# Causal triangle by matmul in two blocks, wide zero matmuls and a new order of work in a fused attention and MLP kernel

## The chip, the cores and the metric

The kernel runs on one core of one Trainium2 chip. A core has five engines that each work through their own list of instructions in order: PE (matmuls; PEld is its loading of weights), ACT (activations and copies), DVE (vector work), POOL (element-wise work, and the issue of software DMAs) and SP (here only the issue of hardware DMAs). Engines wait for each other by semaphores. The metric is the device time of one launch in microseconds (us); lower is better.

## The reference

The inputs are q, k and v of shape (4, 8, 768, 64) and two weight matrices, 512x2048 and 2048x512, all float32. For each query the reference bounds its score against each chunk of 32 keys, keeps the six best chunks among those that causality allows, and runs causal softmax attention over the keys of these chunks. A softplus MLP follows.

```python
k_min, k_max = k_chunks.min(axis=3), k_chunks.max(axis=3)
ub = sum(maximum(q * k_min, q * k_max), axis=-1)   # causal chunks only
top_chunks = argsort(ub)[..., -6:]
scores = where(sel & (pos_q >= pos_k), q @ k.T / 8, -1e9)
attn = softmax(scores)
x = (attn @ v) laid out as (3072, 512)
out = softplus(x @ w_in) @ w_out
```

## The kernel before

The work is cut into 12 blocks of 256 queries: block n is batch n // 3 and query block n % 3, so a block sees 256, 512 or 768 keys. Work on one block has these steps; the names are those of the planned operations, with n the block.

- **Loads.** k and q of block 0 come as f32 by SP's queue (`ld k0`, `ld q0`, line 352) and are cast on ACT or DVE. v of block 0, all of k, q and v of later blocks, and the weights come by POOL's software queue, which casts to bf16 on the way (line 339; w_in line 376, w_out line 383). Issuing one occupies POOL.
- **Preparation.** k and q are turned: in blocks 0 to 2 by PE transposes (`kT`, `qT`, line 471), from block 3 by DMA transposes on SP's queue (line 475). DVE takes maxima and minima of the chunks (`kx`, `kn`), `bd` lays them out, `kc`, `qc` and `qac` copy, `qpn` splits q into positive and negative parts. `ub` (lines 570, 574) is the matmul of the bounds, `mx` the six best, `raw` the mask, `mT` its transpose, `mc` its copy into extra rows beside q. Matching rows beside k (`ohk`, made by POOL as `oh` in lines 275 to 279 and spread by SP) make the score matmul add the mask.
- **Attention.** `s` (lines 687, 688) writes scores of one head against 256 keys; where those are the diagonal keys, its second matmul covers 128 queries only. `ex` (line 695) is the exponential on ACT. On the diagonal `af` (line 705, POOL) then sets to zero what lies above it. `av` (line 717) multiplies with v and a column of ones, `nm` normalizes, `oT` (line 743) or a DMA transpose (line 732) turns the result, and `xc` puts it into x.
- **MLP.** `h` (line 791), exponential `e` (796) and logarithm `ln` (801) on ACT, `y` (816), `ye` copies and `st` stores.

All instructions are put into their lists by a planner that is part of the kernel's program (`Plan.run`). Each operation has a key, and a due time: the smallest of its own key and of the due times of what follows it less durations. A loop keeps a planned time for each engine and each buffer. For each engine it takes, among those operations that could start within a tolerance (`tol`) of the earliest, the one with the smallest due time. DMAs are given a planned time of landing by a small model of the two queues. Keys, tolerances and buffer counts are the numbers in `PAR` (lines 224 to 245). What reaches the chip is the order on each engine, no times: an instruction runs as soon as its engine comes to it and its semaphores are there.

`keep_awake` (line 837) then fills PE's planned idle time in the first 45 us with matmuls of zeros (line 852), each of 128 columns, counted so that they end 60 ns before the planned start of the next real operation. They cost what the planner holds them to cost: 107 ns before 5.7 us and 55.8 ns later. A buffer pool `io` of eight tiles takes the loaded k and q.

Of the kernel before, what the change touches and what calls it, by code (L numbers as in the profile page):

```python
# [21 lines left out]
QB = 256  # L22
# [41 lines left out]

class Op:
    __slots__ = ("name", "alts", "fn", "deps", "gate", "after", "succ", "alloc", "touch", "key",
                 "rel", "packet", "port", "due", "wait", "eng", "start", "end", "done", "dma", "n", "at", "inst")


class Plan:  # L70
# [5 lines left out]
    def op(self, name, alts, fn, deps=(), alloc=(), touch=(), key=None, dma=None, gate=(), after=(), rel=0.0, packet=19.0, port=False):  # L76
        o = Op()
        o.rel, o.packet, o.port = round(rel), packet, port
# [50 lines left out]
    @staticmethod  # L129
    def home_at(pool, s, e):  # L130
        t = 0.0
        for q, x, dma in pool.ends[s]:
            t = max(t, x + (LANDED[e] if dma else 0 if q == e == "PE" else LAT[q].get(e, 150)))
        return t

    def run(self, par):
# [11 lines left out]
        ring, packet = {"SP": 0.0, "POOL": 0.0}, {"SP": 19.0, "POOL": 32.0}  # L148
# [3 lines left out]
        while ready:  # L152
# [26 lines left out]
            if o.dma:  # L179
                other = "SP" if e == "POOL" else "POOL"  # L180
                at = max(o.end + (650 if e == "SP" else 1150), ring[e], 2650.0)
                back, part = max(0.0, ring[other] - at), packet[other] / o.packet
                ring[e] = at + o.dma + min(o.dma * part, back)
                ring[other] += min(o.dma, back / part)
                packet[e] = o.packet
                o.done = ring[e] + (450 if o.packet < 100 else 1000)
                if e == "SP":
                    o.end = max(o.end, ring[e] - 3500)
            else:
                o.done = o.end  # L190
# [4 lines left out]
            for b in o.touch:  # L195
                b.left -= 1
                b.ends.append((e, o.done, bool(o.dma)))
# [22 lines left out]
def dve(n, rate=1.0):  # L220
    return n / (0.96 * rate) + 66


PAR = dict(
    dmat=3,
    dmaT=450,
    narrow=1,
    l0=1,
    over="soy",
    maskD=3,  # L230
    awake=(1.06, 45.0, 5.7),
    first=(64.42, 64.23, 29.03, 95.39),
    loads=((87.43, 130.15, 71.7), 19.14, (76.86, 12.06, 15.17), 41.22),
    tol={"PE": 0, "ACT": 0, "DVE": 0, "POOL": 2358, "SP": 0},
    alt=636,
    ohd=(229.35, 150.58),
    a=(-46.8, -33.92, -31.03, -0.05, 17.1, 24.77, 54.71, 88.7, 133.12, 175.62, 173.66, 255.42, 297.45, 469.8),
    prep=((77.31, -48.97, -81.43, 46.38), (-8.14, 24.92, -67.86, -43.68), (53.78, -16.07, -58.0, 11.26), (25.03, -41.37, -16.45, 11.23)),
    av=(-0.8, 4.76),
    ot=(12.12, 10.86),  # L240
    hlag=(8.7, 27.7, 34.1, -3.53, 34.9, 33.84, 33.54, 32.2, 25.36, -32.32, 54.03, 77.81),
    ylag=(7.32, 7.87, 25.64, 26.35, 28.67, 47.05, 47.88, 49.45, 10.02, 22.03, 47.36, 37.39),
    ahead=(3.4, 19.67, 10.64, 22.05, 12.72, 9.33, 70.63, 47.4, 103.95),
    sizes=dict(s=2, h=2, y=1, o=1, t=2, xf=2, xp=4, kT=2, io=8, kx=2, q=2, pn=2, ub=2, pt=4, osb=4, x=4, g=2, e=4, ysb=4, mT=2),
# [3 lines left out]
def make_plan(T, par):  # L248
# [19 lines left out]
    P.op("zero", [("DVE", 80)], lambda e: nc.vector.memset(T.zero, 0.0), key=-100000)  # L268
# [26 lines left out]
    chunk_rows = [P.op("c4", [("POOL", 900)], f4, [r4], key=3000)]  # L295
    mr0, bd0, kb0, vone, ohk = [], [], [], [], {}
# [11 lines left out]
    for k0, k1 in ((0, 1), (1, NBLK)):  # L308
        for h in range(2):
            o = P.op("ohk", [("SP", 450)], lambda e, k0=k0, k1=k1, h=h: rows_of(0, k0, k1, h), oh[k0:k1],  # L310
                     key=par["ohd"][k0] * 1e3, dma=300 * (k1 - k0))
# [16 lines left out]
    def load(nm, n, when, gate=()):  # L328
# [6 lines left out]
        for t in range(NT):  # L335
# [4 lines left out]
                     gate=gate, key=key, rel=key - 2000 if n > 2 else 0.0, dma=950 if n < 3 else 2050, packet=32.0, **new)  # L340
            first = first or o
            ld[nm, n, t] = o

    def load_pairs(nm, n, when):
# [4 lines left out]
        for g in range(2):  # L349
# [4 lines left out]
                     key=1e3 * when[g], dma=950, packet=29.0, alloc=[st])  # L354
# [6 lines left out]
    def load_rows(nm, n, when):  # L361

        for t in range(NT):
            st = Buf(pool["xf"])
            d = P.op(f"ld {nm}{n}.{t}", [("SP", 560)], lambda e, t=t, st=st: nc.sync.dma_start(out=st.ap, in_=rows(nm, n, t)),
                     key=1e3 * (when + 0.3 * t), dma=1000, alloc=[st])
# [5 lines left out]
    def load_w_in(when):  # L372
        for c in range(4):
# [4 lines left out]
            w_in.append(P.op(f"w_in{c}", [("POOL", 800)], f, key=1e3 * (when + 0.4 * c), dma=2550, packet=173.0, after=w_in[-1:]))  # L378

    def load_w_out(when):  # L380
        for c in range(4):
# [4 lines left out]
            w_out.append(P.op(f"w_out{c}", [("POOL", 800)], f, key=1e3 * (when + 0.4 * c), dma=2550, packet=173.0,  # L386
# [5 lines left out]
    load_pairs("k", 0, (0.0, l0[0]))  # L392
    if par["l0"] < 2:
        load_pairs("q", 0, (l0[1], l0[2]))
    else:
        load("q", 0, l0[1])
# [4 lines left out]
    for nm, x in zip("kqv", l1):  # L401
        load(nm, 1, x)
    load_w_in(li)
    for nm, x in zip("kqv", l2):
        load(nm, 2, x)
    load_w_out(lo)
    for h in range(2):
        o = P.op("ohk", [("SP", 450)], lambda e, h=h: rows_of(1, 0, NBLK, h), oh, gate=[w_out[3]], key=40000, dma=900)
        for k in range(NBLK):
            ohk[1, k, h] = o  # L410
    kb0.append(P.op("kb0", [("SP", 450)], lambda e: nc.sync.dma_start(out=T.KB[1][0:32], in_=T.KB[0][0:32]), kb0[:1],
                    gate=[w_out[3]], key=40000, dma=600))
# [7 lines left out]
    for n in range(NB):  # L420
# [11 lines left out]
        for gi, ps in enumerate(groups):  # L432
# [14 lines left out]
            by_dma, pairs, qpairs = n >= par["dmat"], n == 0, n == 0 and par["l0"] < 2  # L447
# [20 lines left out]
            def transposes(nm, buf, t, n=n, ps=ps, p0=p0):  # L468
                o = t_of(buf)
                for p in ps:  # L470
                    nc.tensor.transpose(o[:, p - p0, t * 128:(t + 1) * 128],
# [476 lines left out]
```

## Time and profile before

| | |
|---|---|
| median of 3 runs | 264.73 us (264.21 to 266.2) |
| profiled execution, its own time | 266.59 us |
| its span | 264.8 us |
| PE, ACT, DVE, POOL busy | 96%, 80%, 54%, 42% of the span |
| mean granted clock of PE | 0.994 |
| first and last matmul of an MLP (lines 791, 816) | start 36.06 us, end about 261.2 us |

The page gives shares of the span. Its tenths are 40 slices of 6.6 us each. Times inside the profile are counted from the span's start, and the profiled execution took 1.8 us more than its span; that execution was itself 1.9 us over the median. A matmul's row is longer than the time to the next one, since matmuls overlap: only distances between starts tell what one costs.

### The profile page before, as it was taken

The numbers are of one execution on the slowest core, as the hardware profiler recorded it, in microseconds if no ns is written. First come the engines' busy times: TensorE is split into PE (matmuls) and PEld (weight loads), VectorE is DVE, ScalarE is ACT, GpSimd is POOL, SyncE is SP. The second block draws the span as 40 slices with busy tenths as digits, with TensorE's granted clock in tenths as the row PEclk, the third lists the DMA queues.
The fourth block names the chain that finished last, engine by engine and source line by source line (L and its number), as shares of the span: only waits on it lengthen the run. The fifth ranks groups of instructions, "written<-read, shape, count | busy, mean of one in ns | idle before, by whom it ended". The sixth has DMA issues, their size and how long they took to land.

```text
span 264.8 us, 7039 instructions
## 1 busy us (share of the span) xinstructions
PE 255.0 (96%) x2750; PEld 197.2 (74%) x2779; DVE 142.5 (54%) x500; ACT 211.0 (80%) x372; POOL 110.8 (42%) x193
## 2 busy tenths in 40 slices
PE   8698999999999999999999999999999999999995
PEld 8698898768775677788678864777888756887744
DVE  6589961019789667447634596584582164221012
ACT  3589999988687879999687992699997885999900
POOL 8927878798318520543990263401110211310000
PEclk9799999999999999999999999999999999999999
DMA  7996999999999984699699969624440123001022
GB/s 162 161 189 90 181 196 231 155 139 190 149 136 173 132 119 89 115 129 100 73 173 150 117 88 174 173 54 120 45 82 0 42 72 99 10 2 42 0 79 79
DMA packets 114719, 29.87 MB, mean 113 GB/s; under 512 B 104544, under 2 KB 111712, under 8 KB 114688
## 3 DMA queue, kind: packets, MB, share of 16 engines
q0 software_dynamic: 74944, 13.11, 66.5%
q1 hardware_dynamic: 39744, 16.33, 33.0%
q8 instruction: 21, 0.34, 0.6%
q14 instruction: 10, 0.08, 0.1%
HBM read 27.26 MB, written 6.29 MB: 127 GB/s over the span
## 4 chain that ended last, share of the span: by engine, by line
PE 86%; DMA 5%; DVE 3%; ACT 3%; issue 1%; POOL 0%; DVEq 0%; POOLq 0%
PE ph L791 30%; PE py L816 17%; PE pt L816 9%; PE po L717 7%; PE ps L687 5%; PE py L852 4%; PE ps L688 4%; DMA io<-in_k_dram 3%; DMA x<-osb 3%; PE pt L687 2%; PE pt L688 1%; PE pt L570 1%; ACT g L801 1%; PE ph L816 1%; ACT e L796 1%
## 5 line engine op out<-in xcount | busy, mean ns | idle before, releaser
L791 PE MATMUL ph<-x,w_in_sb 128*128 128x256 bf16 x768 | 91.8, 272 | 0.0
L705 POOL TENSOR_SCALAR_AFFINE_SELECT pt<-pt 128x256 bf16<-128x256 bf16 x96 | 39.5, 419 | 112.6 <-ACT pt L695 112.1
L791 PEld LDWEIGHTS <-w_in_sb 128*128 128x128 bf16 x768 | 73.6, 98 | 11.5 <-DMA w_in_sb<-in_moe_w_in_dram 0.5
L695 ACT ACTIVATE pt<-ps 128x512 bf16<-128x512 f32 (+1 forms) x134 | 69.9, 564 | 9.4 <-PE ps L688 8.8
L796 ACT ACTIVATE e<-ph 128x512 f32<-128x512 f32 x96 | 56.3, 606 | 12.5 <-PE ph L791 11.8
L816 PEld LDWEIGHTS <-g 128*128 128x128 bf16 x400 | 37.4, 98 | 31.4 <-ACT g L801 0.5
L816 PE MATMUL py<-w_out_sb,g 128*128 128x512 bf16 x231 | 57.8, 379 | 1.5 <-ACT ysb L258 0.2
L801 ACT ACTIVATE g<-e 128x1024 bf16<-128x1024 f32 x48 | 51.1, 1072 | 1.0
L695 ACT ACTIVATE pt<-pt 128x512 bf16<-128x512 f32 (+1 forms) x58 | 32.4, 584 | 0.6 <-PE pt L688 0.6
L717 PEld LDWEIGHTS <-pt 128*128 128x128 bf16 x672 | 26.8, 97 | 5.1 <-issue 0.6
L259 DVE COPY ysb<-py 128x512 f32<-128x512 f32 x12 | 8.3, 691 | 36.9 <-PE py L816 36.9
L717 PE MATMUL po<-v,pt 128*128 128x65 bf16 x610 | 26.4, 193 | 0.3 <-DVE osb L728 0.3
L816 PE MATMUL pt<-w_out_sb,g 128*128 128x512 bf16 x108 | 26.2, 379 | 0.2
L727 DVE RECIPROCAL rec<-po 128x4 f32<-128x4 f32 x43 | 7.6, 178 | 34.9 <-PE po L717 34.6
L490 DVE TENSOR_REDUCE kx<-kT 128x32 bf16<-128x1024 bf16 x18 | 21.0, 1209 | 8.9 <-DMA kT<-io 8.9
L852 PE MATMUL py<-zero 128*128 128x128 bf16 x243 | 22.7, 245 | 1.1 <-DVE zero L268 1.1
L339 POOL DMA_DIRECT2D v<-in_v_dram x24 | 21.6, 905 | 3.8 <-DMA io<-in_q_dram 1.5
L339 POOL DMA_DIRECT2D io<-in_k_dram x22 | 20.0, 910 | 5.7 <-DMA w_in_sb<-in_moe_w_in_dram 2.2
L339 POOL DMA_DIRECT2D io<-in_q_dram x22 | 19.9, 910 | 0.7 <-PE ph L791 0.6
L728 DVE TENSOR_TENSOR osb<-po,rec 128x256 bf16<-128x256 f32 x43 | 18.2, 424 | 2.7 <-DMA x<-osb 1.3
L852 PEld LDWEIGHTS <-zero 128*128 128x128 bf16 x243 | 18.3, 111 | 1.3 <-DVE zero L268 1.1
L687 PE MATMUL ps<-qa,ka 96*128 96x256 bf16 x71 | 18.3, 273 | 0.7 <-DVE qa L259 0.7
(99 smaller groups left out, 302.5 us busy)
## 6 DMA issues: line engine op xcount, KB each, us to landing
out_dram<-ysb SPq DMA_DIRECT2D x23, 256.0 KB, 2.4
v<-in_v_dram POOLq DMA_DIRECT2D x24, 128.0 KB, 7.6
io<-in_k_dram POOLq DMA_DIRECT2D x22, 128.0 KB, 7.2
io<-in_q_dram POOLq DMA_DIRECT2D x22, 128.0 KB, 7.1
w_out_sb<-in_moe_w_out_dram POOLq DMA_DIRECT2D x4, 512.0 KB, 8.0
w_in_sb<-in_moe_w_in_dram POOLq DMA_DIRECT2D x4, 512.0 KB, 9.6
xp<-in_k_dram SPq DMA_DIRECT2D x2, 256.0 KB, 3.2
xp<-in_q_dram SPq DMA_DIRECT2D x2, 256.0 KB, 6.3
```

What stands on the lines that cost most here:

```text
L339: lambda e, t=t: nc.gpsimd.dma_start(out=into(nm, n, t), in_=rows(nm, n, t)),
L490: nc.vector.tensor_reduce(kx.ap[:, :, j].rearrange("d p (t c) -> d t p c", t=NT), kT.ap.rearrange("d p x -> d (p x)").rearrange("d (t p c ...
L687: nc.tensor.matmul(sp.ap[:, 0:QB], kk[0:nr, p, j * 128:(j + 1) * 128], qq, start=True, stop=True)
L695: lambda e, sp=sp, pt=pt, h=h, j=j, w=w: nc.scalar.activation(pt.ap[:, h, j:j + 2].rearrange("k j c -> k (j c)")[:, 0:w], sp.ap[:, 0:w], A ...
L705: nc.gpsimd.affine_select(out=d, in_=d, compare_op=ALU.is_ge, fill=0.0, base=0, channel_multiplier=-1, pattern=[[0, 2], [1, 128]])
L717: nc.tensor.matmul(o[:, u, h], pt.ap[:, h, j, c0:c0 + 128], T.V[i][:, j, 2 * p + h, :], start=(j == 0), stop=(j == t0 + u))
L728: nc.vector.tensor_tensor(osb.ap[0], o[:, :, :, 0:D], osb.ap[1].to_broadcast([128, NT, 2, D]), op=ALU.mult)
L791: nc.tensor.matmul(o[:, j], T.w_in[:, dt, ft * 128:(ft + 1) * 128], x.ap[:, dt], start=(dt == 0), stop=(dt == KDM - 1))
L796: lambda e, hb=hb, eb=eb, f2=f2: nc.scalar.activation(eb.ap[:, f2 * 512:(f2 + 1) * 512], hb.ap, ACT.Exp),
L801: lambda e, eb=eb, g=g, f4=f4: nc.scalar.activation(g.ap[:, f4 * 4:(f4 + 1) * 4].rearrange("f j c -> f (j c)"), eb.ap, ACT.Ln, bias=1.0),
L816: nc.tensor.matmul(yb.ap[:, 0:c1 - c0], g.ap[:, f, u * 128:(u + 1) * 128], T.w_out[:, f, c0:c1], start=(f == 0), stop=(f == KFF - 1))
L852: z.fn = lambda e: T.nc.tensor.matmul(T.pools["y"].homes[0][:, 0:128], T.zero, T.zero, start=True, stop=True)
```

## The change

Seven things change.

1. **Triangle.** In blocks 0 and 1 (`tri=2`) the causal triangle is added before the exponential: behind each of the two diagonal score matmuls stands a 128x128 matmul of the identity with a constant tile `tri` that holds a large negative number above the diagonal. The `af` selections of these two blocks go, 8 per block. Other blocks keep them. POOL makes `tri` from zeros that DVE writes.
2. **Software loads.** In the plan no software load of blocks 0 to 2 begins ahead of 3.3 us (`rel=3300`). No wait in the kernel goes with it.
3. **Zero matmuls.** They take 512 columns, and 128 where 512 no longer fit. The tile of zeros has 512 columns.
4. **Model of the DMAs.** The class `Rings` takes the place of a few lines: packets of two queues share the engines, a software transfer waits for hardware ones issued before it for up to 3.3 us, and a transfer lands later than its last packet by an amount of its own (`land`): 0.45 us for f32 loads, 1.3 to 3.2 us for software loads (`SKEW` for block 0), 2.8 us for transposes. It sets only the order.
5. **Due times.** `tweak` adds to an operation's due time by its name. Among some 170 entries: tri -1.15, `ld q1.0` -3.0, `ld k1.1` -30.76, `ld v0.0` +19.38, vone +18.65, oh +19.6.
6. **Numbers.** All keys are new, POOL's tolerance goes from 2.36 us to 9.85 us.
7. **Buffers.** `io` goes from eight tiles to five.

A loader `load_both` and its transposes are added too; with `both=0` nothing calls them.

```diff
+class Rings:
+    def __init__(self):
+        self.t, self.q, self.on = 0.0, {"POOL": [], "SP": []}, {"POOL": False, "SP": False}
+        self.slots = []
+    def run(self, until, ends):
+        t, q, on = self.t, self.q, self.on
+        pair = (("POOL", "SP"), ("SP", "POOL"))
+        while True:
+            nxt = 1e18
+            for e, f in pair:
+                if q[e] and not on[e]:
+                    x = q[e][0]
+                    late = x[1] + 3300.0
+                    if x[1] <= t and (t >= late or not q[f] or q[f][0][5] > x[5]):
+                        on[e] = True
...
+            per = sum(q[e][0][4] for e in act)
+            if len(act) == 2:
+                per += q["SP"][0][0].pen
...
+    def add(self, o, now):
+        self.run(max(now, self.t), [])
+        e = "POOL" if o.eng == "POOL" else "SP"
...
+        self.q[e].append([o, max(o.end + (1150 if e == "POOL" else 650), 2650.0), n, 0, o.packet, o.end])
...
@@ Plan.run
+        for o in topo:
+            o.due += 1e3 * par["tweak"].get(o.name, 0.0)
...
-                at = max(o.end + (650 if e == "SP" else 1150), ring[e], 2650.0)
...
-                o.done = ring[e] + (450 if o.packet < 100 else 1000)
+                for x, y in rings.add(o, t - 2500.0):
+                    y += x.land
...
@@ PAR
+    tri=2,
-    first=(64.42, 64.23, 29.03, 95.39),
-    loads=((87.43, 130.15, 71.7), 19.14, (76.86, 12.06, 15.17), 41.22),
-    tol={"PE": 0, "ACT": 0, "DVE": 0, "POOL": 2358, "SP": 0},
+    first=(93.07, 179.76, 83.28, 50.42),
+    loads=((108.73, 142.65, 46.12), 80.17, (59.6, 38.68, 238.83), 28.45),
+    tol={"PE": 27, "ACT": 222, "DVE": 0, "POOL": 9847, "SP": 0},
-    a=(-46.8, -33.92, -31.03, -0.05, 17.1, 24.77, 54.71, 88.7, 133.12, 175.62, 173.66, 255.42, 297.45, 469.8),
-    prep=((77.31, -48.97, -81.43, 46.38), (-8.14, 24.92, -67.86, -43.68), (53.78, -16.07, -58.0, 11.26), (25.03, -41.37, -16.45, 11.23)),
-    av=(-0.8, 4.76),
-    ot=(12.12, 10.86),
+    a=(-77.41, -53.74, -51.32, -48.9, 23.04, 68.67, 100.01, 106.1, 141.55, 250.15, 284.3, 344.37, 488.94, 634.54),
+    prep=((58.7, -107.29, -20.36, 94.1), (40.17, 56.54, -119.0, -8.26), (-6.33, -38.41, -55.12, -66.62), (19.56, -17.84, 30.35, -49.53)),
+    av=(-16.58, 36.73),
+    ot=(-42.75, -53.14),
...
@@ make_plan
+    if par["tri"]:
+        t0_ = P.op("tri0", [("DVE", 100)], lambda e: nc.vector.memset(T.tri, 0.0), key=2000)
+        tri_ = [P.op("tri", [("POOL", 430)], lambda e: nc.gpsimd.affine_select(
+            out=T.tri, in_=T.tri, compare_op=ALU.is_ge, fill=NEG, base=0, channel_multiplier=-1, pattern=[[1, 128]]), [t0_], key=8000), ident]
...
-                     gate=gate, key=key, rel=key - 2000 if n > 2 else 0.0, dma=950 if n < 3 else 2050, packet=32.0, **new)
+                     gate=gate, key=key, rel=key - 2000 if n > 2 else 3300.0 if par["l0"] == 1 else 0.0, dma=850, packet=13.3, land=(SKEW if n == 0 else 2200.0 if n == 1 else 3200.0 if n < 9 else 1500.0), **new)
...
-                        nc.tensor.matmul(sp.ap[:, 0:QB], kk[0:nr, p, j * 128:(j + 1) * 128], qq, start=True, stop=True)
-                        nc.tensor.matmul(sp.ap[:, QB:w], kk[0:nr, p, (j + 1) * 128:(j + 2) * 128],
-                                         qq[:, 1] if last else qq, start=True, stop=True)
+                        add = last and tri
+                        for c0, c1, x in ((0, QB, qq), (QB, w, qq[:, 1] if last else qq)):
+                            jj = j + c0 // QB
+                            nc.tensor.matmul(sp.ap[:, c0:c1], kk[0:nr, p, jj * 128:(jj + 1) * 128], x, start=True, stop=not add)
+                            if add:
+                                nc.tensor.matmul(sp.ap[:, c0:c0 + 128], T.ident, T.tri, start=False, stop=True)
...
-                    if last:
+                    if last and not tri:
                         def f_a(e, pt=pt, h=h, t0=t0):
...
@@ keep_awake
-    fill, free = [], 1e3 * par["awake"][0]
+    fill, free = [], max(1e3 * par["awake"][0], 140 + next(o.end for o in order if o.name == "zero"))
...
-            c = 107 if t < 1e3 * par["awake"][2] else mm(128)
-            if t + c > o.start - 60:
-                break
...
+        for w in (512, 128):
+            while True:
+                c = w / 1.2 if t < 1e3 * par["awake"][2] else mm(w)
+                if t + c > o.start - 60:
+                    break
...
```

More of the change, by code (lines that the diff above doesn't have):

```diff
@@ L65 @@
 class Op:
     __slots__ = ("name", "alts", "fn", "deps", "gate", "after", "succ", "alloc", "touch", "key",
-                 "rel", "packet", "port", "due", "wait", "eng", "start", "end", "done", "dma", "n", "at", "inst")
+                 "rel", "packet", "port", "land", "pen", "due", "wait", "eng", "start", "end", "done", "dma", "n", "at", "inst")
 class Plan:
@@ L377, in f @@
                                            in_=T.moe_w_in[:, fs].rearrange("(kt ki) f -> ki kt f", ki=128))
-            w_in.append(P.op(f"w_in{c}", [("POOL", 800)], f, key=1e3 * (when + 0.4 * c), dma=2550, packet=173.0, after=w_in[-1:]))
+            w_in.append(P.op(f"w_in{c}", [("POOL", 800)], f, key=1e3 * (when + 0.4 * c), dma=2550, packet=80.0, land=3300.0, after=w_in[-1:]))
     def load_w_out(when):
@@ L411, in make_plan @@
     kb0.append(P.op("kb0", [("SP", 450)], lambda e: nc.sync.dma_start(out=T.KB[1][0:32], in_=T.KB[0][0:32]), kb0[:1],
[L412 removed]
+                    gate=[w_out[3]], key=40000, dma=520, packet=260.0, land=2000.0))
     for n in range(3, NB):
```

179 lines of the change are left out of this document (123 added, 56 removed).

## The prediction

> **What bounds the kernel now.** The page comes first. PE is busy for nearly the whole span.
>
> ```profile
> span 264.8 us, 7039 instructions
> PE 255.0 (96%) x2750; PEld 197.2 (74%) x2779; DVE 142.5 (54%) x500; ACT 211.0 (80%) x372; POOL 110.8 (42%) x193
> ```
>
> That share counts matmuls of zeros and overlapping rows, so I ask how much is useful. Weight loads by line, in three stretches, first for the zeros (line 852); the number behind x is the count.
>
> ```profile
> 0.00:20.00 20.00, 11.11 (x130) 0.91 1.54 171
> 20.00:40.00 20.00, 6.68 (x107) 1.00 1.09 156
> 40.00:261.00 221.00, 0.46 (x6) 1.00 0.96 104
> ```
>
> The zeros stop at 40 us. From there to 261 us the same view gives, for lines 791, 816, 717, 687 and 688 in this order:
>
> ```profile
> 40.00:261.00 221.00, 72.19 (x752) 1.00 0.96 104
> 40.00:261.00 221.00, 37.20 (x398) 1.00 0.96 104
> 40.00:261.00 221.00, 23.36 (x592) 1.00 0.96 104
> 40.00:261.00 221.00, 15.99 (x165) 1.00 0.96 104
> 40.00:261.00 221.00, 16.18 (x166) 1.00 0.96 104
> ```
>
> The chain of waits prices a matmul by long undisturbed pieces (start, us, what):
>
> ```profile
> 20.76 1.40 PE py L852 x25
> 63.23 0.66 PE po L717 x22
> 79.10 1.73 PE py L816 x8
> 199.94 6.99 PE ph L791 x64
> ```
>
> So 56 ns for 128 columns, 30 for line 717, 216 for 512 columns, 109 for 256. Then 752 x 109 = 82.0 us; line 816 has 32 half-width ones, 366 x 216 + 32 x 109 = 82.5; 592 x 30 = 17.8; 165 x 109 = 18.0; line 688 has half its matmuls at 128 columns, 166 x 82 = 13.6. Together 214 of 221 us, and 162 small ones (lines 570, 743) take about 4 more. **From 40 us PE has no slack**: at most 3 us can be won there, and whatever is added there is paid in full. Behind the last matmul stand a copy and a store that the change doesn't touch.
>
> What can be won lies in the first 40 us, where 237 zero matmuls stand. The timeline of PE shows how it begins:
>
> ```profile
> 6.15 1.11 PE L852 MATMUL py<-zero 128*128 128x128 bf16 x11
> 9.50 0.62 PE L471 MATMUL ph<-ident,io 128*128 128x128 bf16 x8 [2.24 <-DMA io<-in_k_dram]
> 9.96 2.39 PE L852 MATMUL py<-zero 128*128 128x128 bf16 x23
> 12.13 0.63 PE L471 MATMUL ph<-ident,io 128*128 128x128 bf16 x4
> 12.56 0.63 PE L471 MATMUL pt<-ident,io 128*128 128x128 bf16 x4
> 12.99 0.63 PE L852 MATMUL py<-zero 128*128 128x128 bf16 x4
> 13.41 0.22 PE L570 MATMUL ph<-bd,qpos 128*128 128x16 bf16 x1
> ```
>
> The counts of zeros keep the plan's times. Eleven at 56 ns from 6.15 say that block 1's k was planned for about 6.8; it came for 9.50: 2.7 us late. Then 31 matmuls planned at 1.73 took 12.13 - 9.50 = 2.63, and 12 planned at 0.67 took 13.41 - 12.13 = 1.28. **The list slipped 2.7 + 0.9 + 0.6 = 4.2 us**, and since the zeros are executed whether needed or not, and nothing has slack after 40 us, the end slipped with it.
>
> The two later pieces ran slowly for this reason (windows of 2 us; the number behind the busy times is PE's granted clock):
>
> ```profile
> 10.00:12.00 2.00, 2.00 (x25) 2.00 (x22) 1.11 (x4) 1.83 (x4) 2.00 (x3) 0.56 2.42 161
> 12.00:14.00 2.00, 2.00 (x33) 2.00 (x31) 1.19 (x1) 1.06 (x3) 2.00 (x4) 0.59 2.09 168
> ```
>
> The clock fell to 0.56 and 0.59 behind a wait of 2.24 us. The Trainium skill ("TensorE: Matmul & The Clock Gate", the section on the HAM clock gate) has PE fall to half rate after an idle window of about 3.4 us; by it this wait would be too short, the slow stretch would not be its doing, and the gain below would be 1.5 us smaller. The row is nearer, and I keep 4.2.
>
> **The change, part by part.** Late data first: could those 4.2 us be had, or does the work wait for DVE and ACT anyway?
>
> ```profile
> 4.00:36.00 32.00, 28.54 (x451) 26.30 (x448) 26.40 (x100) 26.02 (x46) 24.06 (x42) 0.95 1.43 161
> 1.85 1.06 SPq L352 DMA_DIRECT2D xp<-in_q_dram x2
> 2.08 1.90 POOL L339 DMA_DIRECT2D io<-in_k_dram x2
> 1.73 0.70 DVE L270 MEMSET ohb<- 32x768 bf16 x1
> 3.84 0.62 ACT L258 CAST io<-xp 128x512 bf16<-128x512 f32 x1 [1.75 <-DMA xp<-in_k_dram]
> 4.72 0.62 ACT L258 CAST io<-xp 128x512 bf16<-128x512 f32 x1 [0.26 <-DMA xp<-in_k_dram]
> 7.67 0.62 ACT L258 CAST io<-xp 128x512 bf16<-128x512 f32 x1 [2.33 <-DMA xp<-in_q_dram]
> ```
>
> DVE is busy 26.4 of these 32 us and ACT 26.0, so a better start is worth at most about 5.6 us unless work is reordered. q of block 0, asked for at 1.85, came for 7.67, while block 1's loads, issued from 2.08, shared the engines. If these begin at 3.3 instead, 1.2 us later, q keeps the engines to itself longer. The two pieces of k before it came 0.9 us apart (casts at 3.84 and 4.72), so q's first piece could land near 5.6: 2.1 us earlier. Block 1's k was there just before 9.50 and will hardly be earlier, but an order that expects it there fills PE, DVE and ACT with block 0 meanwhile. Bounds of this part: 0 (the slip returns elsewhere) and 5.6. I take 3.5, nearer to the measured slip.
>
> Does POOL wait till 3.3 us at all? No semaphore makes it. By the due times of the code, as I work them through, `ident` and `c4` come first as now (to 2.08), then `tri`, due 3 us ahead of `ld q1.0`, then q1.0, k1.0, k1.1, q1.1, v. `tri` waits for zeros that DVE writes behind the memset of ohb, which ends at 2.43 here; with both memsets and the selection itself POOL reaches the loads at an estimated 3.1.
>
> The triangle takes 16 selections from POOL:
>
> ```profile
> L705 POOL TENSOR_SCALAR_AFFINE_SELECT pt<-pt 128x256 bf16<-128x256 bf16 x96 | 39.5, 419 | 112.6 <-ACT pt L695 112.1
> 20.07 0.78 POOL L705 TENSOR_SCALAR_AFFINE_SELECT pt<-pt 128x256 bf16<-128x256 bf16 x2 [4.76 <-ACT pt L695]
> 27.55 0.77 POOL L376 DMA_DIRECT2D w_in_sb<-in_moe_w_in_dram x1
> 34.64 0.64 ACT L258 COPY x<-pt 128x256 bf16<-128x256 bf16 x2
> 36.06 1.03 PE L791 MATMUL ph<-x,w_in_sb 128*128 128x256 bf16 x8
> ```
>
> 16 x 0.419 = 6.7 us of POOL go, and the wait of 4.76 us at 20.07, behind which v of block 1 and w_in stood. The new due times put w_in ahead of w_out and right behind v, so it is issued before 20 us instead of 27.55. The first matmul of the MLP at 36.06 now needs x (34.64 + 0.64 = 35.28) and w_in; with w_in early, x alone decides, and the new keys ask for block 0's `oT` ahead of blocks 1 and 2. MLP work gives PE more per time of ACT than scores do, so an early MLP fills what zeros hold: 107 zeros x 56 ns = 6.0 us from 20 to 40. Bounds 0 and 6.0; I take 2, because ACT is full from 16 us on and the early MLP delays exponentials.
>
> On PE come 32 matmuls of 128 columns, 32 x 56 ns = 1.8 us. Beside zeros they cost nothing, past 40 us all of it; the scores of block 1 end about there, so 0.3. A pair's `av` is released some 0.4 us earlier without `af`; that is inside the 2.
>
> At nothing: wide zeros (a count for a planned time, whatever the width; if the plan is late they delay real work, a rival below); the memset of 512 columns (0.1 us longer, PE's first zero moves with it and nothing waits); the model, tolerances and keys themselves, which only order; five `io` tiles. Those hold two and a half blocks:
>
> ```profile
> 39.00 1.77 POOL L339 DMA_DIRECT2D io<-in_k_dram  x2 [0.42 <-issue]
> 49.48 1.35 SPq L475 DMA_TRANSPOSE kT<-io x1
> kT<-io SPq DMA_TRANSPOSE x9, 8.5
> ```
>
> A tile lives from 39.00 to about 49.48 + 8.5 = 58, 19 us, and a block lasts 221 / 12 = 18.4 us, so two to three tiles are in use. If loads were late, each us would be paid in full; I allow that in the range.
>
> **Sum**: 3.5 + 2 - 0.3 = 5.2 us less. The profiled execution took 266.6 us (1.8 around its span): 261.4. The median of the runs is 1.9 below it: **259.5 us**, 2% faster.
>
> **The rivals.**
>
> *Gained, then given back* (within 1%). Loads, transposes and weights of blocks 3 to 5 come as they do now, and a PE that is 5 us ahead waits for them. For it speaks a piece of the chain, and the page's row of DMA, full till about 92 us:
>
> ```profile
> 87.22 7.05 DMA x<-osb
> DMA  7996999999999984699699969624440123001022
> ```
>
> The chain went through a transpose there while PE had other work. Against it: the fall to 6 in the fifth slice (20 to 26 us) is POOL's wait, which goes, so the stream moves forward too. Price: the 5.2 less the 1 us or so of later start that the stream recovers: 263.5 us.
>
> *The plan is too cautious* (slower). Place: PE's list before 40 us. Zeros hold PE to the plan, so each us that the plan expects a landing (2.2 us behind the last packet for block 1) too late is a us lost, as 4.2 were lost the other way. It decides for slower when the first MLP matmul starts later than now, 36.06. With landings planned 2 us late in two stages and blocks 1 and 2 behind them, it starts at about 40: 264.7 + 4 = 268.7 us. For it: measured time from issue to landing varies by load, so a plan can't be right for all; against it: the present plan erred towards early.
>
> *Software loads are not held* (the change doesn't do what it says): if `tri` stands behind the loads, they go at 2.1 as now, q comes for 7.67 and the slip keeps 2.1 of its 3.5: 261.6 us.
>
> By the same page of the Trainium skill, section "Back-to-back issue gap", a stream of load and matmul at 128 columns takes 81 ns each; the triangle would then be 2.6 us, not 1.8, and the sum the same to 0.3 us. The row of 25 zeros in 1.40 us says 56.
>
> **How the numbers follow.** The forecast (257 to 261.5) 0.48; loads not held 0.12; given back 0.18; too cautious 0.22. What a measurement of this kernel can tell from no change is about 1%, 2.6 us, so from 262.1 to 267.4 is the same. Faster: 0.48 and most of 0.12, 0.58; slower: most of 0.22, 0.18; same 0.24. The range runs from the forecast with both upper bounds nearly had (8.5 less: 256.2) to 267.5, which leaves out the worse part of the slower rival.
>
> **What would show it.** In the profile of the changed kernel: the first software load at 3 us or later, q's first cast before 6.5; no wait of PE over 1 us and no granted clock under 0.9 between 6 and 14 us; no line 705 on POOL before 36 us and no POOL wait of 4 us; w_in issued before 20; the first matmul of line 791 before 32; fewer than 13 us of zeros; as much useful work per us after 40 us as now. The prediction is wrong if the first MLP matmul doesn't come earlier, or if it does and PE then shows waits between 40 and 100 us.

## The result, and the profile after

The changed kernel takes **267.07 us** (266.26 to 268.88, 18 runs) where the kernel before takes 264.78 (263.68 to 266.6, 18 runs): ratio **1.0085, 95% interval 1.0063 to 1.0107**. That is 2.3 us slower. The prediction's own bound of 1% calls this no change, though the interval lies wholly above 1. It forecast 259.5. The profiled execution after took 266.49 us.

The page after, its span, its first group and the row of DMA:

```profile
span 264.8 us, 6772 instructions
PE 252.6 (95%) x2609; PEld 187.0 (71%) x2642; DVE 136.3 (51%) x489; ACT 215.8 (81%) x382; POOL 104.6 (39%) x180
DMA  7999999999999959197321299997631211003112
```

PE is as full as before, and its clock was not halved in the start: the windows of 2 us that stood at 0.56 and 0.59 before now show 1.00 (the number behind the five engines).

```profile
10.00:12.00 2.00, 1.84 (x41) 1.54 (x40) 1.76 (x12) 1.45 (x3) 1.81 (x5) 1.00 2.13 136
12.00:14.00 2.00, 2.00 (x21) 1.22 (x20) 1.91 (x10) 1.24 (x3) 1.93 (x4) 1.00 0.98 84
```

The start does what was forecast. The timeline after (start, us, engine, line, what, wait and its releaser), first POOL's software loads, ACT's casts of the f32 data, PE's first `ub` and its first MLP matmuls:

```profile
2.78 0.29 POOL L373 TENSOR_SCALAR_AFFINE_SELECT tri<-tri 128x128 bf16<-128x128 bf16 x1 [0.56 <-DVE tri L372]
3.02 1.01 POOL L418 DMA_DIRECT2D io<-in_q_dram  x1
17.21 0.76 POOL L469 DMA_DIRECT2D w_in_sb<-in_moe_w_in_dram  x1
3.87 0.62 ACT L332 CAST io<-xp 128x512 bf16<-128x512 f32 x1 [1.78 <-DMA xp<-in_q_dram]
6.57 0.62 ACT L332 CAST io<-xp 128x512 bf16<-128x512 f32 x1 [1.23 <-DMA xp<-in_k_dram]
10.43 0.17 PE L678 MATMUL pt<-bd,qpos 128*128 128x16 bf16 x1
28.36 1.03 PE L903 MATMUL ph<-x,w_in_sb 128*128 128x256 bf16 x8
```

`tri` holds POOL, the first software load starts at 3.02, the first `ub` comes 3.0 us earlier than before (13.41), the first MLP matmul 7.7 us earlier (36.06). So the time must be lost later. PE's windows (busy us and count of PE, PEld, DVE, ACT, POOL, then clock, DMA share, GB/s) say where. Before:

```profile
70.00:90.00 20.00, 19.68 (x171) 13.61 (x173) 16.89 (x50) 15.86 (x29) 9.92 (x17) 1.00 1.75 147
110.00:250.00 140.00, 139.02 (x1463) 106.25 (x1479) 68.68 (x250) 117.88 (x211) 42.66 (x78) 1.00 0.71 86
```

After:

```profile
50.00:70.00 20.00, 19.89 (x234) 15.10 (x235) 11.66 (x27) 18.36 (x34) 15.76 (x22) 1.00 2.12 161
70.00:90.00 20.00, 17.48 (x154) 11.88 (x156) 14.57 (x57) 15.78 (x28) 12.24 (x20) 1.00 2.13 164
110.00:250.00 140.00, 138.97 (x1429) 104.11 (x1447) 63.35 (x227) 118.69 (x215) 41.47 (x78) 1.00 0.61 83
```

**Between 70 and 90 us PE stands 2.5 us**, where it stood 0.3 before; from 50 to 70 and from 110 on it is full. PE's waits there, in the timeline after:

```profile
74.22 0.19 PE L678 MATMUL pt<-bd,qneg 128*128 128x32 bf16 x1 [0.96 <-ACT qneg L655]
81.04 0.33 PE L799 MATMUL ps<-qa,ka 96*128 96x256 bf16 x2 [0.19 <-DVE qa L333]
81.93 0.33 PE L799 MATMUL ps<-qt,kb 128*128 128x256 bf16 x2 [0.56 <-DVE qt L333]
87.10 0.81 PE L928 MATMUL py<-w_out_sb,g 128*128 128x512 bf16 x3 [0.59 <-ACT g L913]
```

These are the selection of block 4 (`ub`), the scores of block 3, which wait for mask rows (`qa` and `qt`), and an MLP matmul that waits for its logarithm. Back along that chain, SP's and POOL's timelines after:

```profile
50.62 6.04 SPq L583 DMA_TRANSPOSE kT<-io  x2
57.95 0.35 SPq L939 DMA_DIRECT2D out_dram<-ysb  x1
59.66 5.83 SPq L583 DMA_TRANSPOSE qt<-io  x2
73.15 1.19 SPq L744 DMA_TRANSPOSE mT<-mraw  x1
28.92 0.88 POOL L418 DMA_DIRECT2D io<-in_q_dram  x1 [0.23 <-issue]
34.84 0.87 POOL L418 DMA_DIRECT2D io<-in_k_dram  x1 [1.95 <-PE po L829]
47.05 0.78 POOL L817 TENSOR_SCALAR_AFFINE_SELECT pt<-pt 128x256 bf16<-128x256 bf16 x2 [11.34 <-ACT pt L807]
47.90 0.89 POOL L418 DMA_DIRECT2D io<-in_q_dram  x1
48.79 1.76 POOL L418 DMA_DIRECT2D io<-in_k_dram  x2
53.54 1.77 POOL L418 DMA_DIRECT2D io<-in_q_dram  x2
```

and SP's before:

```profile
55.35 1.34 SPq L475 DMA_TRANSPOSE qt<-io  x1
60.98 0.35 SPq L827 DMA_DIRECT2D out_dram<-ysb  x1
68.75 1.19 SPq L636 DMA_TRANSPOSE mT<-mraw  x1
```

The loads at 28.92 to 34.84 are block 4's. Then POOL stands 11.34 us for block 2's first exponential, and **block 3's q and k stand behind it**: they go out at 47.90 to 54.4, where the k of block 3 went out at 39.00 before. Block 3's mask transpose follows at 73.15, 4.4 us later than before, although PE's work is ahead: the second store goes out at 57.95 against 60.98, 3.0 us earlier, and the order that asks for the MLP sooner flatters even that.

### The profile page after: what moved, and what is told of

Read it like the earlier page. It is cut to its first block, busy times and chain, and to the rows that moved or that the text cites. A ratio compares the mean times of both kernels' runs of the same rounds, so it can differ in the third digit from the quotient of the medians.

```text
span 264.8 us, 6772 instructions
## 1 busy us (share of the span) xinstructions
PE 252.6 (95%) x2609; PEld 187.0 (71%) x2642; DVE 136.3 (51%) x489; ACT 215.8 (81%) x382; POOL 104.6 (39%) x180
## 3 DMA queue, kind: packets, MB, share of 16 engines
q1 hardware_dynamic: 39744, 16.33, 28.7%
## 4 chain that ended last, share of the span: by engine, by line
PE 73%; ACT 10%; DMA 8%; DVE 3%; POOL 3%; issue 2%; SPq 0%; ACTq 0%; DVEq 0%; POOLq 0%
PE ph L903 25%; PE py L928 16%; PE pt L928 9%; PE ps L799 8%; PE po L829 5%; PE pt L799 4%; DMA io<-in_k_dram 3%; DMA kT<-io 3%; ACT pt L807 2%; ACT qt L332 2%; DMA xp<-in_k_dram 2%; ACT g L913 1%; POOL io L418 1%; PE ph L928 1%; PE pt L829 1%
## 5 line engine op out<-in xcount | busy, mean ns | idle before, releaser
L903 PE MATMUL ph<-x,w_in_sb 128*128 128x256 bf16 x768 | 93.4, 272 | 0.6 <-ACT e L908 0.6
L817 POOL TENSOR_SCALAR_AFFINE_SELECT pt<-pt 128x256 bf16<-128x256 bf16 x80 | 31.9, 415 | 95.2 <-ACT pt L807 95.0
L928 PE MATMUL py<-w_out_sb,g 128*128 128x512 bf16 x233 | 59.1, 379 | 1.8 <-ACT g L913 0.6
L913 ACT ACTIVATE g<-e 128x1024 bf16<-128x1024 f32 x48 | 49.8, 1062 | 0.8
L807 ACT ACTIVATE pt<-pt 128x512 bf16<-128x512 f32 (+1 forms) x56 | 29.9, 581 | 2.3 <-PE pt L799 1.7
L829 PE MATMUL po<-v,pt 128*128 128x65 bf16 x560 | 24.3, 193 | 0.1
L799 PE MATMUL ps<-qt,kb 128*128 128x256 bf16 (+1 forms) x136 | 23.3, 259 | 0.9 <-DVE qt L333 0.6
L799 PE MATMUL ps<-qa,ka 96*128 96x256 bf16 (+1 forms) x136 | 23.0, 257 | 0.9 <-ACT pt L807 0.5
L799 PEld LDWEIGHTS <-ka 96*128 96x128 bf16 x192 | 17.2, 97 | 4.3 <-issue 1.0
L799 PEld LDWEIGHTS <-kb 128*128 128x128 bf16 x192 | 16.4, 97 | 4.8 <-issue 1.0
## 6 DMA issues: line engine op xcount, KB each, us to landing
w_out_sb<-in_moe_w_out_dram POOLq DMA_DIRECT2D x4, 512.0 KB, 13.8
```

What stands on the lines that cost most here:

```text
L799: nc.tensor.matmul(sp.ap[:, c0:c1], kk[0:nr, p, jj * 128:(jj + 1) * 128], x, start=True, stop=not add)
L807: lambda e, sp=sp, pt=pt, h=h, j=j, w=w: nc.scalar.activation(pt.ap[:, h, j:j + 2].rearrange("k j c -> k (j c)")[:, 0:w], sp.ap[:, 0:w], A ...
L817: nc.gpsimd.affine_select(out=d, in_=d, compare_op=ALU.is_ge, fill=0.0, base=0, channel_multiplier=-1, pattern=[[0, 2], [1, 128]])
L829: nc.tensor.matmul(o[:, u, h], pt.ap[:, h, j, c0:c0 + 128], T.V[i][:, j, 2 * p + h, :], start=(j == 0), stop=(j == t0 + u))
L903: nc.tensor.matmul(o[:, j], T.w_in[:, dt, ft * 128:(ft + 1) * 128], x.ap[:, dt], start=(dt == 0), stop=(dt == KDM - 1))
L913: lambda e, eb=eb, g=g, f4=f4: nc.scalar.activation(g.ap[:, f4 * 4:(f4 + 1) * 4].rearrange("f j c -> f (j c)"), eb.ap, ACT.Ln, bias=1.0),
```

## The experiments

**Theory A**: the lead of the first 40 us is given back because block 3's data come late, through the order of the queues. Its rivals: the triangle's matmuls or another single part of the change cost the time; five `io` tiles hold the loads up; the order of blocks doesn't matter, because ACT and DVE or the transfers as a whole set the pace there (**B**, **C**).

Each kernel ran beside the kernel before. Ratios to it, with their intervals, and PE's busy time from 70 to 90 us in the profiled execution:

| kernel | ratio (95%) | PE busy, 70 to 90 |
|---|---|---|
| after | 1.0085 (1.0063 to 1.0107) | 17.48 |
| `before2` | one execution: 265.51 us | 19.68 |
| `b_wide` | 0.9943 (0.9917 to 0.9969) | 19.68 |
| `b_tri` | 0.9971 (0.9946 to 0.9995) | 19.68 |
| `b_both` | 0.9985 (0.9960 to 1.0011) | 19.68 |
| `b_hold` | 1.0006 (0.9977 to 1.0035) | 19.68 |
| `a_notri` | 1.0104 (1.0040 to 1.0167) | 16.80 |
| `a_io8` | 1.0162 (1.0106 to 1.0218) | 18.33 |
| `a_early3` | 1.0051 (1.0016 to 1.0085) | 17.29 |
| `a_light` | 1.0231 (1.0185 to 1.0277) | not used |
| `a_swap34` | 1.0101 (1.0060 to 1.0141) | 19.10, and 16.99 from 50 to 70 |
| `a_fix3` | 1.0043 (1.0010 to 1.0075) | 19.31 |
| `a_light2` | 1.0072 (1.0042 to 1.0102) | 17.23 |

**The kernel before, once more (`before2`)**, unchanged.

> The kernel before once more, for a second profile. The first profile was of an execution of 266.6 us, 1.8 above the median. If the late landing of block 1's k (9.50, PE idle for 2.24 us) belongs to every execution, it is here too and PE's useful work begins at the same times to 0.5 us. If it belongs to that execution, PE waits under 1 us between 6 and 10 us here, the granted clock stays above 0.9, and the time is nearer to 264.7.

Its timeline of PE:

```profile
8.85 0.62 PE L471 MATMUL ph<-ident,io 128*128 128x128 bf16 x8 [2.56 <-DMA io<-in_k_dram]
9.31 1.45 PE L852 MATMUL py<-zero 128*128 128x128 bf16 x23
11.26 0.17 PE L570 MATMUL ph<-bd,qpos 128*128 128x16 bf16 x1
```

The k is late again, by 8.85 - 6.8 = 2.05 us, but the 23 zeros behind the wait take 56 ns each: no half clock. (It is block 2's k, not block 1's as the prediction has it: the kernel's first software load is `ld k2.0`, and the planner lists `kT2` at this place.) The first `ub` comes at 11.26, not 13.41. So of the slip of 4.2 us that the prediction read, this execution has about 2; the rest is a landing that was 0.65 us later and the half clock, which comes in some executions only (last section). Its second store goes out at 59.55 and its mask transpose at 67.25: against this execution the lead of the changed kernel at 58 us is 1.6 us at most, and its block 3's mask is 5.9 us later.

**The parts, each alone in the old order.**

```
b_tri   + matmul(sp, ident, tri) behind the last scores of a head, n < 2;  - affine_select, n < 2
b_wide  zeros 512 columns wide where the gap has room
b_both  the two together
b_hold  POOL: the first one-hot selection and a memset ahead of the first software load
```

> The kernel before, in its own order, with the triangle of blocks 0 and 1 added by matmul (32 more matmuls, 16 selections fewer on POOL, two small POOL instructions more at the start). The prediction's reasoning: POOL's wait of 4.76 us at 20 us goes, v and w_in go out earlier; the MLP starts earlier by up to 3 us only if the order lets it, which it does not here, so -0.5 to +0.3: 264.3 to 265.1. If the matmuls are paid in full and POOL's relief is worth nothing: +1.8: 266.6.

> The kernel before with its zeros 512 columns wide where a gap has room, order unchanged. Predicted at nothing: within 0.5 us of the kernel before, 264.3 to 265.3. Rival: wide zeros hold real work back where data come early, or keep the clock up where 128 columns do not: then 1 us or more either way.

> The kernel before in its own order, with the triangle of blocks 0 and 1 by matmul and with wide zeros together. If the two small gains (ratios 0.9971 and 0.9943) add: 0.990 to 0.993, 262.0 to 262.9 where the kernel before takes 264.7. If both come from the same early microseconds (the start at half clock and the wait for late data): 0.994 to 0.996.

> The kernel before with its first software load held back by 1.7 us (the first one-hot selection and a memset of POOL put ahead of it), all else in the old order. The prediction's theory (the software loads slow the f32 loads, which are what the start waits for): q of block 0 is cast before 6.5 instead of 7.67, but block 1's k comes no earlier, and PE's list, which asks for it at 6.8, still slips: 0 to -1 us, ratio 0.996 to 1.000. Rival: the software loads are what the start waits for; held by 1.7 us they make the first ub matmul 1 to 1.7 us later, ratio 1.003 to 1.007.

None of the parts costs time. The triangle is 0.3% faster, the wide zeros 0.6%; together they come to 0.15%, with an interval that holds 1, so the small gains don't add and `b_both` lies above both its expectations. Against the 0.85% of the whole change, **the loss must be in what is left of it, the new order with its five tiles**, or in how the parts act inside that order. `b_hold` comes near the first theory: the ratio is a little above the range named, which its interval holds. Its q is cast earlier (`b_hold`, then the same cast in `before2`, in fences of their own), its first `ub` is hardly earlier (11.10 against 11.26), and the time is the same.

```profile
6.28 0.62 ACT L258 CAST io<-xp 128x512 bf16<-128x512 f32 x1 [0.97 <-DMA xp<-in_q_dram]
```

```profile
7.00 0.62 ACT L258 CAST io<-xp 128x512 bf16<-128x512 f32 x1 [1.78 <-DMA xp<-in_q_dram]
```

**The triangle taken out of the changed kernel (`a_notri`)**; the causal triangle inside blocks 0 and 1 is then not applied.

```
-  add = last and tri
+  add = False
```

> The changed kernel without its 32 triangle matmuls, order unchanged; the causal triangle inside blocks 0 and 1 is left out of the computation. If the triangle is paid in full (32 x 56 ns = 1.8 us on a PE without slack): 265.3. If it stands beside zeros or waits, as predicted (0.3): 266.8. By theory A, where a lead at 40 us is lost again to late data of block 3, a lead won here is lost too: 266.5 to 267.1.

1.0104, with a wide interval: 1.8 us less than the changed kernel would be 1.0017, which lies outside it. Either the matmuls stood beside zeros, or what they free is lost again; its PE is busy only 18.49 us from 50 to 70 and 16.80 from 70 to 90. So the triangle is not the cause. Which of the two holds isn't shown.

**Eight `io` tiles (`a_io8`)**, same order, tiles taken in turn.

```
+  for b, i in fresh.items(): b.slot = i % 8
```

> The changed kernel with the same order on every engine and eight io tiles instead of five. Theory tiles: POOL's waits for transposes between 60 and 80 us (8.8 us) go, loads of later blocks come earlier, 1.5 to 2.5 us less. Theory order and theory bandwidth: POOL's waits go but block 3's loads still stand behind the selections, so within 0.7 us of 267.1.

Slower, and in a new place. POOL now waits for a tile only once (4.71 us at 72.60; 16.7 us in all in the changed kernel), so most loads of block 11 go out at 163.78 to 167, together with block 9's transposes; in the changed kernel they follow from 170.26 on. DVE then waits for block 9's k, and PE behind it:

```profile
173.99 2.35 DVE L598 TENSOR_REDUCE kx<-kT 128x32 bf16<-128x1024 bf16 x2 [3.71 <-DMA kT<-io]
178.08 0.17 PE L678 MATMUL pt<-bd,qpos 128*128 128x16 bf16 x1 [2.50 <-DVE bd L333]
```

Five tiles are not what holds block 3: its q still goes out at 47.77, behind a wait of 12.41 us for the exponential. That they do the kernel good by holding later loads back fits this profile, but was not tried alone.

**Block 3's loads ahead of POOL's long wait (`a_early3`).**

```
   ld k4.1
+  ld q3.0, ld k3.0, ld k3.1, ld q3.1
   affine_select of block 2 (waits for the exponential)
```

> The changed kernel with one edit in POOL's list: the four loads of block 3's q and k are issued ahead of the selections of block 2, for which POOL waited 11.3 us (35.7 to 47.05), not behind them. Theory order (block 3 is late because its loads stood behind that wait): block 3's mask transpose is issued 4 us or more before the 73.15 of the changed kernel, PE's lost time between 70 and 90 us (2.7 us) falls under 1.2, and the time falls by 1.5 to 2.5 us to some 265. Theory bandwidth (the DMA engines are full up to 86 us whatever the order): no change, 267.1 within 0.7. Theory tiles (five io tiles): no change.

The wait changes its reason and not much of its length: in both kernels block 3's loads may not go out before the last piece of w_out has landed. The change sends three pieces of w_in and three of w_out from 21.59 to 28.7, and a piece of w_out takes 13.8 us from issue to landing in the median, 8.0 before.

```profile
44.44 0.87 POOL L418 DMA_DIRECT2D io<-in_q_dram  x1 [9.64 <-DMA w_out_sb<-in_moe_w_out_dram]
71.61 1.35 SPq L744 DMA_TRANSPOSE mT<-mraw  x1
```

The loads are 3.5 us earlier, the mask 1.5, where theory order had named 4 or more. PE's 70 to 90 us stay as in the changed kernel (17.29), so there was more between the loads and the mask. The ratio can't be told from 1.0085.

**Less of w_out, first try (`a_light`)**: a quarter of pieces 1 to 3 loaded, the rest set to zero, so the second MLP matmul lacks most of its sum.

```
   ld k4.1
+  nc.gpsimd.memset(T.w_out[:, c * 4 + 1:(c + 1) * 4, :], 0.0)
```

> The changed kernel with the same order and less to load: of the last three quarters of w_out only every fourth tile is loaded (1.1 MB less, some 6 us of the DMA engines at 190 GB/s), the rest is zeros that POOL writes while it waits anyway. Left out: three quarters of three quarters of w_out. Theory bandwidth: what follows comes up to 6 us earlier, PE's lost time between 70 and 90 us goes, 2 to 2.5 us less. Theory order: POOL still waits till about 47 us with block 3's loads behind, no more than 0.7 us less.

It tells nothing of the transfers: the memsets themselves took POOL from 34.14 for 4.03 us, and its wait for the exponential ended at 53.25 (47.05). The kernel `a_light2` below does it without them.

**Blocks 3 and 4 exchanged (`a_swap34`).**

```
POOL  q3.0 k3.0 v2.1 k3.1 q3.1 | wait | q4.0 k4.0 k4.1 ... q4.1     no wait for w_out
SP    kD3 qD3 kD4                 DVE  kx3 kn3 bd3 kc3 kx4 kn4 ...
```

> The changed kernel with the roles of blocks 3 and 4 exchanged in its first loads: q and k of block 3 are issued where q and k of block 4 stood (28.9 to 36 us) and the other way round, with the two pairs of io tiles exchanged, without block 3's wait for the last piece of w_out, and with the transposes and the first vector work of block 3 ahead of block 4's. Nothing else moves. Theory A (the lead of the first 40 us is given back because block 3's data come late): block 3's mask transpose goes from 73.15 to 69 or earlier, the 2.65 us that PE loses between 70 and 90 shrink to under 0.8, and the time falls by 1.5 to 2.7 us, to 264.4 to 265.6. Rival B (those 2.65 us are lost to ACT, DVE or a full DMA stream, whichever block comes first): the loss stays within 1 us of 2.65, or moves to block 4's scores, and the time stays within 0.7 us of the changed kernel's 267.1.

Block 3's data are there early, and its mask is later than in the changed kernel, 76.66. SP issued its k transpose only behind the first store (50.78), and on DVE the reduction of block 4 stood ahead of block 3's selection and waited for k of block 4, now the late one:

```profile
66.71 2.35 DVE L598 TENSOR_REDUCE kx<-kT 128x32 bf16<-128x1024 bf16 x2 [3.77 <-DMA kT<-io]
69.67 0.40 PE L855 MATMUL pt<-ident,osb 128*128 128x128 bf16 x2 [2.90 <-DVE osb L840]
76.66 1.50 SPq L744 DMA_TRANSPOSE mT<-mraw  x1
```

Both theories missed: the loss neither shrank nor stayed where it was, it moved to 60 to 70 us. Early data were worth nothing here while the other queues kept the old order.

**Block 3 first in every queue (`a_fix3`).**

```
as a_swap34 on POOL, and
SP    qD3 kD3 | store of block 0 | kD4 ...
DVE   kx3 kn3 bd3 kc3 qac3 uba3 mx3 raw3 | kx4 kn4 bd4 ...
```

> As a_swap34 (block 3's q and k loaded in the places of block 4's, no wait for w_out), and in addition the transposes of block 3's k and q on SP ahead of the first store of output, and all of block 3's selection on DVE ahead of block 4's first reduction. In a_swap34 these two queues kept block 3 waiting: its k transpose was issued only behind the store (50.78), and block 4's reduction, for data that were now late, stood on DVE ahead of block 3's selection (mask transpose at 76.66). Theory A (late data of block 3 give the lead back, each time through one in-order queue): block 3's mask transpose before 71, PE's loss from 60 to 90 us falls from 2.65 to under 1, time 1.5 to 2.5 us below the changed kernel: ratio to the kernel before 0.999 to 1.003. Rival B (the transfers as a whole are too slow there: engines busy from 7 to 92 us, so whichever block comes second is late): the loss from 60 to 110 us stays 2 us or more, now in front of block 4's or 5's work, ratio 1.005 to 1.015.

Its timeline (SP's two transposes and a wait of PE for block 6), and its windows:

```profile
69.44 1.22 SPq L744 DMA_TRANSPOSE mT<-mraw  x1
95.51 3.19 SPq L583 DMA_TRANSPOSE qt<-io  x1
102.77 0.18 PE L678 MATMUL pt<-bd,qpos 128*128 128x16 bf16 x1 [0.58 <-DVE qpos L659]
```

```profile
70.00:90.00 20.00, 19.31 (x190) 13.79 (x192) 15.91 (x52) 17.39 (x32) 14.74 (x23) 1.00 2.15 169
90.00:110.00 20.00, 19.11 (x209) 15.24 (x209) 14.07 (x62) 16.69 (x29) 4.31 (x9) 1.00 0.66 97
```

**The mask is 3.7 us earlier, and 1.8 of the 2.2 us come back between 70 and 90 us.** Theory A's mask (before 71) and its loss of PE from 60 to 90 us (under 1; 0.75) came as named, rival B's loss of 2 us from 60 to 110 did not (1.64). The ratio falls from 1.0085 to 1.0043, just outside the range that theory A had named; the two intervals overlap a little, so it is the windows that show the cause, not the ratio alone. Some 0.8 us are lost anew from 90 to 110, in front of block 6, whose q transpose goes out at 95.51 behind two stores.

**Less of w_out, without memsets (`a_light2`)**: the second MLP matmul uses one loaded 128-row part of each of the pieces 1 to 3 four times.

```
-  T.w_out[:, c * 4:(c + 1) * 4, :]
+  T.w_out[:, c * 4:c * 4 + (1 if c else 4), :]
```

> The changed kernel with a quarter of the second, third and fourth piece of w_out loaded (one of four 128-row parts; the second matmul of the MLP uses that part four times, so its result is another one), order and instruction counts unchanged. Some 2.4 MB of f32 reading leave the transfers ahead of 45 us. Theory C (the transfers are full, and block 3's loads and transposes are slow because of what stands before them): the last piece lands before 38 instead of 44.4, SP's one-hot rows go out before 38, block 4's loads land early, block 3's mask transpose comes at 70 or earlier instead of 73.15, PE's loss of 0.9 at 45 to 50 and 2.65 at 70 to 90 falls below 1.3 in sum: ratio 0.996 to 1.001. Theory A alone (POOL's wait for block 2's first exponential sets when block 3's loads go out, whatever the transfers do): q of block 3 still goes out at 47 to 54, the mask transpose stays at 72 to 74, and the loss at 70 to 90 stays above 2: ratio 1.005 to 1.010.

Theory A alone. The transfers are nearly idle just when POOL waits (windows, GB/s last; then the timeline of POOL and SP):

```profile
40.00:45.00 5.00, 5.00 (x44) 4.03 (x43) 0.84 (x2) 3.45 (x8) 0.00 (x0) 1.00 0.48 99
45.00:50.00 5.00, 4.66 (x32) 2.94 (x32) 0.69 (x1) 5.00 (x10) 3.07 (x5) 1.00 0.15 12
```

```profile
46.86 0.78 POOL L818 TENSOR_SCALAR_AFFINE_SELECT pt<-pt 128x256 bf16<-128x256 bf16 x2 [12.10 <-ACT pt L808]
72.21 1.28 SPq L745 DMA_TRANSPOSE mT<-mraw  x1
```

12 GB/s where the changed kernel moves 166, and block 3's loads still go out at 47.72 and its mask at 72.21. So it is not a full stream of transfers ahead of block 3's loads that makes them late, it is **POOL's own order**.

## Why the prediction was wrong, and where it was right

- *What bounds the kernel.* Right. Before and after, PE is full from 110 us on (139.0 of 140). What the prediction took from this is that little can be won after 40 us; that as much can be lost there it kept for the rivals and the range.
- *The slip of 4.2 us, of which 3.5 can be had.* The mechanism was right (late k, zeros executed all the same), the block was not (it is block 2's k, whose load the new order sends behind block 1's), and **the size was not**. `before2` shows a slip of about 2, and the changed kernel's first `ub` leads it by 11.26 - 10.43 = 0.8 us. 1.5 of the 4.2 were half clock, which a third of the executions of the kernel before show (27 of 81). The prediction then took the full gain off the median of the runs, though most of them don't have that loss.
- *Is POOL held?* Right, by the very wait named (`tri`, 2.78, loads from 3.02). q's first cast came at 3.87, partly because q now goes out first; k's came at 6.57.
- *POOL's relief and w_in, 2 us.* The steps happened: none of the causal selections on POOL before 47.05, the first w_in at 17.21 (the other three from 21.59, later than forecast), the MLP from 28.36, 39 wide and 30 narrow zeros where 243 narrow ones stood. The sign "no POOL wait of 4 us" failed: the wait of 4.76 us at 20 us is gone, but a longer one, 11.34 us, ends at 47.05. The gain is inside the 1.6 us that the lead is at most, and none of it arrives.
- *The triangle at 0.3.* Right as far as it can be seen: `b_tri` is no slower, and `a_notri` no faster.
- *Wide zeros at nothing, five tiles at nothing.* Right as to harm: `b_wide` is even 0.6% faster, and eight tiles are worse.
- *"The model, tolerances and keys themselves, which only order", at nothing.* **This is the step that failed.** The new order costs PE 2.2 us between 70 and 90 us (17.48 busy, 19.68 before), more than the lead of at most 1.6 us. It puts block 3's loads behind block 4's first ones, behind the last piece of w_out (there at 44.44 in `a_early3`) and behind block 2's first selections, for which POOL stood 11.34 us; each of these two waits holds them without the other (`a_early3`, `a_light2`). `a_fix3` takes block 3's work out from behind both, on three queues, and 1.8 of the 2.2 us come back. Which of the new numbers made this order no run shows. POOL's tolerance of 9.85 us alone did not: worked through with the old 2.36 and all else new, the planner still lists block 3's loads behind these selections, and only loads of block 4 move ahead of them.
- *The rivals.* "Gained, then given back" named what happened: a PE that is ahead waits for blocks 3 to 5. Its price was wrong, because it let these loads come as before or earlier; block 3's k went out 9.8 us later (48.79 for 39.00). "Too cautious" gives 268.7, close to the time, but its condition (first MLP matmul after 36.06) is not met, 28.36. The forecast's own test, waits of PE between 40 and 100 us with an earlier MLP, is the one that struck.
- *The Trainium skill's rules.* With the one on the clock gate the gain would have been 1.5 us smaller. That was the better term for the median, since most executions don't have the half clock, but not for its reason: the half clock did follow that wait (last section). The one on 81 ns per matmul isn't borne out: `before2` runs 23 zeros with their weight loads in 1.28 us (9.31 to 10.59), 56 ns each.

Open: the two profiled executions, after and `before2`, differ by 1.0 us (266.49 and 265.51) where the medians differ by 2.3, so more than half of that is seen in no profile. `a_fix3` is still 0.4%, 1.1 us, above the kernel before. The 0.8 us that it loses anew from 90 to 110 us are the nearest candidate, but that was not tried; and its profiled execution, at 265.21 us, is no longer than that of `before2` (265.51), so the profiles alone don't show the rest. Two of its twelve executions have a mean clock of 0.992 (267.27 and 268.28 us), which the changed kernel's don't. Nor was the wait for w_out's last piece taken out alone. `b_wide` and `b_tri` are the versions that beat both kernels; they are 0.6% and 0.3% below the kernel before. Why wide zeros help in the old order was not followed up.

## What to carry to other kernels

On engines that work in order, a wait that is written into the list is a wait for everything behind it: when an order is changed, read each long planned pause and list what stands behind it, on every queue that the data pass (here POOL, SP and DVE; with POOL's list mended alone, `a_early3`, PE lost as much as without). A gain read from one profiled execution should be looked for in a second one before it is taken off a median. And when time is won early in a kernel whose main engine is full, the question is which data must come earlier too for the lead to survive.

## What the runs showed of the hardware

PE's granted clock falls to half behind some waits of 2 to 3 us and not behind others. It fell behind 2.24 us (before), 2.50 us (`a_io8`) and 2.90 us (`a_swap34`), not behind 2.56 us (`before2`). The windows of `a_io8`, whose wait ended at 178.08:

```profile
178.00:180.00 2.00, 1.63 (x22) 1.15 (x22) 1.90 (x7) 0.00 (x0) 0.00 (x0) 0.68 1.57 152
180.00:182.00 2.00, 2.00 (x8) 0.99 (x7) 1.24 (x14) 1.11 (x2) 0.00 (x0) 0.50 1.39 120
182.00:184.00 2.00, 2.00 (x12) 0.87 (x11) 0.00 (x0) 1.12 (x2) 0.00 (x0) 0.97 0.90 82
```

A mean clock of c over 2 us, made of full and half rate, means 2 x 2 x (1 - c) us at half rate: here 4 x (0.32 + 0.50 + 0.03) = 3.4 us; the two windows before, 0.56 and 0.59, give 4 x (0.44 + 0.41) = 3.4 us too. So such a wait costs 1.7 us more than itself where PE is full, and costs it in some executions only: of the 81 executions of the kernel before that stand in the ratios of the experiments, 27 show a mean granted clock of 0.991 to 0.994, and these took 266.11 us in the median, the other 54 265.01. None of the changed kernel's 18 does (0.998 or more); 3 of 6 of `a_io8` do, and 6 of 11 of `a_swap34`.

Which waits do it can be read from the moments at which the clock changes. Within one execution they lie whole multiples of 3.413 us apart: 10.25 and 13.66 us before; 37.41, 44.23, 88.61 and 92.02 us in `a_light`, which is 2, 13 and 1 of them. So time is cut into stretches of that length, wherever the kernel's work lies; in kernels where it doesn't fall, they are counted from the moment at which the trace first records the full clock. PE's busy time in one of them, out of 3.41 us, and the clock in the next:

| kernel | stretch (us) | PE busy | clock in the next |
|---|---|---|---|
| `a_swap34` | 66.28 to 69.69 | 0.51 | half |
| `a_io8` | 175.31 to 178.72 | 0.62 | half |
| `a_light` | 85.19 to 88.61 | 1.02 | half |
| before | 6.83 to 10.25 | 1.18 | half |
| `a_light` | 33.99 to 37.41 | 1.45 | half |
| `a_early3` | 79.77 to 83.18 | 1.62 | full |
| `b_hold` | 6.30 to 9.71 | 1.73 | full |
| `before2` | 7.18 to 10.59 | 1.74 | full |

In these traces the border lies between 1.45 and 1.62 us of work in 3.41. The wait of 2.56 us in `before2` is longer than the 2.24 before, but a boundary at 7.18 cuts it into 0.89 and 1.67; the 2.24 lie within one stretch.

The Trainium skill ("TensorE: Matmul & The Clock Gate", "Part 1: The HAM clock gate") has an activity window of 3413 ns that runs freely, and half rate after at least one idle window. The distances agree with the window's length and with its running freely. That the window must be idle as a whole doesn't agree: the clock fell behind stretches with up to 1.45 us of work in them.
